# Attention: row maxima transposed in halves, sums of values in column blocks, sign bits scaled by ScalarE

## The chip, the core and the metric

One kernel runs on one core of a Trainium2 chip. The metric is the device time of one execution in microseconds. The core has five engines that matter here: TensorE (PE; its weight loads are the rows PEld), VectorE (DVE), ScalarE (ACT), GpSimd (POOL) and SyncE (SP, which issues DMAs). Each works through its own queue in program order and waits on semaphores for the others.

## The reference

A bucketed attention over 4 x 8 heads of 768 rows, followed by a routed layer of eight experts. The change touches attention alone.

```python
q_bits = (np.einsum('bhsd,dk->bhsk', q, proj) > 0).astype(np.int64)
k_bits = (np.einsum('bhsd,dk->bhsk', k, proj) > 0).astype(np.int64)
q_bucket = np.sum(q_bits * powers, axis=-1)      # powers = 2 ** np.arange(6)
k_bucket = np.sum(k_bits * powers, axis=-1)
mask = q_bucket[:, :, :, None] == k_bucket[:, :, None, :]
scores = scale * np.matmul(q, k.transpose(0, 1, 3, 2))
scores = np.where(mask, scores, -1000000000.0)
scores = scores - np.max(scores, axis=-1, keepdims=True)
attn = np.exp(scores)
attn = attn / (np.sum(attn, axis=-1, keepdims=True) + 1e-09)
return np.matmul(attn, v).astype(np.float32)
```

The result, as 3072 rows of 512, goes to the experts: each takes 384 rows by a greedy assignment over logits, and computes `relu(x @ w1) @ w2`.

## The kernel before

Heads are worked on in eight groups of four; a group `G` has its query, key and value tiles (`qp`, `kp`, `vp`), their f16 high parts (`qh`, `kh`, `vh`) and low parts (`ql`, `kl`, `vl`), and the operands `QA`, `KA`, `QB`, `KB` (two sets, alternating by group), in which the rows 64 to 69 hold sign bits times 4096 and rows from 96 on the row maxima. Signs of 4096 make equal buckets the only ones that count.

A head passes through two matrix products of the same scores:

- The **S pass** (`S_pass`, lines 231 to 238). For each of six blocks of 128 query rows, TensorE makes scores of 128 x 770 in a buffer of the pool `psS` (two buffers of two PSUM banks each), and VectorE reduces them to the negated maximum, a column of the tile `m6`.
- The **transposed scores** (`ST`, lines 255 to 262), one step later for use: for each of six blocks of 128 keys, in two halves of 384 queries, two matmuls (L260, L261) into a buffer of the pool `psT` (three buffers of one bank), and ScalarE's exponential into `pt`. GpSimd, for about a quarter of the blocks VectorE, subtracts the bf16 high part (`lo`, L265), and four steps later `AV` (L275 to L277) multiplies by the values, 18 matmuls.

Between them stands `m_rows` (lines 240 to 251): the six columns of `m6` are broadcast and transposed by six matmuls with an identity (L245), and ScalarE writes the rows from 96 on of `QA` from them (L246), which `ST` of that head reads. For the heads from 2 on the six matmuls go into one buffer of `psS`, between two S passes; for the heads 0 and 1 in halves into `psT` (L248 to L251).

Sign bits (`bits`, lines 130 to 143): f32 matmuls in four column blocks of 32 into a buffer of `psS`; VectorE compares with zero (L142) and scales by 8192 (L143). `moves` sends bits and operands through SyncE's DMA queue.

The sum of all values of a head (`sumv`, lines 195 to 210) is needed for rows that match nothing. For the groups 0 to 2 it is twelve matmuls of `vh` and `vl` with the constant `on` (L207); for the groups 3 to 7 VectorE first sums over blocks (`colsum`, L194, four per group) and one f32 matmul with `onf` follows (L202). ScalarE and VectorE then write `wf` (L209, L210).

The order is written out by hand. A step `t` runs `ST` half 0, the S passes due, the extras of slot `2t`, `ST` half 1, `lo`, the extras of slot `2t+1`, and `AV`; in one step of six `AV` stands at the step's start instead. `add(n, f, ...)` puts an extra into a slot, by the numbers of the table `AP`. S passes run nine steps ahead of `ST`. `m_rows` of a head stands two slots after its last S pass, which is behind the first S pass of the next head; the matmuls of `xtr` (L302, transposes of finished output for the logits) use `psT` too.

Of the kernel before, what the change touches and what calls it, by code (L numbers as in the profile page):

```python
# [8 lines left out]
F32 = mybir.dt.float32  # L9
F32R = mybir.dt.float32r  # L10
F16 = mybir.dt.float16
BF = mybir.dt.bfloat16
I32 = mybir.dt.int32
AF = mybir.ActivationFunctionType
# [9 lines left out]
 MR=2,  # L24
# [9 lines left out]
 EA=[(0,0),(0,0),(307,4)],  # L34
 RV=[14,3],
 MV=[28, 59, 96, 1],
 CL=9,
 WS=-23,
 SU=14,
 OPS='b0 i3 i2 t0 b1 w5 r0 r2 w4 s0 w4 C1 r1 t1 c1 s1 B0 c0 D0 w2 w1 s4 w5 s2 s3 r3 v2 w5 v0 l0 l1 C0 m0 s5 w3 s6 r5 w2 l3 e0 e1 d0 u0 u1 s7 v1 l2 w0 m1 e2 | s8 | x0 | w0 | x1 s9 | r4 s10 | | | s11 m2 v3 f0 | x3 | | x2 | m3 | | | | | |')  # L40
# [4 lines left out]
def attention(tc, nc, ctx, qT, kT, vv, proj, wg, x_dram, L, jp, identf, B, late=None, after=None):  # L45
# [64 lines left out]
    wc=row(97,768.0,"wc"); ml=row(98,-1.0,"ml")  # L110
    on=cp.tile([128,128],F16,name="on"); G_.memset(on,0.0); G_.memset(on[:,97:99],1.0)
    onf=cp.tile([128,128],F32,name="onf"); late=[lambda: G_.memset(onf,0.0),lambda: G_.memset(onf[:,97:99],1.0)]+list(late or ())
    ident=cp.tile([128,128],F16,name="ident"); V.tensor_scalar(ident,jp,0.0,None,op0=ALU.is_equal)
# [16 lines left out]
    def bits(G,pairs):  # L130
        if (G,'b') not in TMP: TMP[G,'b']=dp.tile([128,S],F16,name="bt",bufs=1)
        bt=TMP[G,'b']; r=slice(0,128)
        ps=psS.tile([128,2,512],F32,name="pss")
        for hf in range(2):
            if G==0:
                for w in range(2):
                    T.matmul(ps[32*w:32*w+32,hf,0:384],pr[0:64],(qd,kd)[w][0:64,1,hf*384:hf*384+384],start=True,stop=True,tile_position=(0,32*w))
            for p in pairs:
                for w in range(2):
                    cg=64*p+32*w  # L140
                    T.matmul(ps[cg:cg+32,hf,0:384],pr,LD[G][w][:,p,hf*384:hf*384+384],start=True,stop=True,tile_position=(0,cg))
        V.tensor_scalar(bt.rearrange("p (z q) -> p z q",z=2),ps[:,:,0:384],0.0,0.5,op0=ALU.is_gt,op1=ALU.subtract)  # L142
        V.tensor_scalar(bt[r],bt[r],8192.0,None,op0=ALU.mult)  # L143
    def dm(G,pairs,eng=SY):
# [45 lines left out]
    def sv(G,j,e=None): (e or V).tensor_tensor(VL[G%2][:,j],LD[G][2][:,j],VH[G%2][:,j,:,0:64],op=ALU.subtract)  # L190
    SV={}
    def colsum(G,j):
        if j==0: SV[G]=dp.tile([128,4,64],F32,name="sv",bufs=1)
        V.reduce_sum(SV[G][:,j],LD[G][2][:,j].rearrange("p c d -> p d c"),axis=AX.X)  # L194
    def sumv(G):
        u=G%2
        if G<2:
            A.copy(WF[u][96:128,:,64],wc[96:128,:].to_broadcast([32,4]))
        ps=psT.tile([128,512],F32,name="pst")
        pv=ps[96:128,0:256].rearrange("p (j d) -> p j d",j=4)  # L200
        pa=ps[:,0:256].rearrange("p (j d) -> p j d",j=4)
        if G in SV: T.matmul(pa,onf,SV[G],start=True,stop=True)  # L202
        else:
            n=0
            for c in range(6):
                for src in (VH[u],VL[u]):
                    T.matmul(pa,on,src[:,:,c,0:64],start=n==0,stop=n==11,skip_group_check=True); n+=1  # L207
        hi=dp.tile([128,4,64],F16,name="shi",bufs=1)
# [31 lines left out]
    def m_rows(h,hf):  # L240
        G,j=divmod(h,4)
        if h>=2:
            ps=psS.tile([128,2,512],F32,name="pss")
            for c in range(6):
                T.matmul(ps[:,c//3,c%3*128:c%3*128+128],M6[h][:,c:c+1].to_broadcast([128,128]),ident,start=True,stop=True)  # L245
            A.activation(QA[G%2][96:128,j,:].rearrange("p (z q) -> p z q",z=2),ps[96:128,:,0:384],AF.Relu,bias=mbi[96:128],scale=msc[96:128])  # L246
            return
        MR[hf]=psT.tile([128,512],F32,name="pst")  # L248
# [68 lines left out]
    def add(n,f,*a): at.setdefault(n,[]).append((f,a))  # L317
# [9 lines left out]
    for o in AP['OPS'].split():  # L327
# [3 lines left out]
        if o[0]=='e': early.append(int(o[1:]))  # L331
    add(AP['WS'],wsplit); add(AP['SU'],sumv,0)
    for G in range(1,NG):
# [5 lines left out]
        for n in range(4): add(p[8+n],sub,G,n%2,n//2)  # L339
        add(p[12],bits,G,[0,1]); add(AP['MV'][G-1] if G<4 else 48*(G-1)+AP['MV'][3],moves,G)  # L340
        for j in range(4): add(p[15]+st*j,cv,G,j); add(p[15]+st*j+sg,sv,G,j,G_)
        if G>2:
            for j in range(4): add(p[18]-AP['RV'][0]+AP['RV'][1]*j,colsum,G,j)
        add(p[18],sumv,G)
        if G>1: add(48*(G-1)+AP['CL'],clear,G)

    k=12; done={}; S_at={}
    for t in range(6*NH):
        while k<min(6+(AP['S'][0]*t+AP['S'][1])//6,t+1+LEAD,6*NH):
            S_at.setdefault(t,[]).append(divmod(k,6)); done[k//6]=t; k+=1  # L350
    for h in range(2,NH):
        add(2*done[h]+AP['MR'],m_rows,h,0)
    for h in range(1,NH,2):
# [5 lines left out]
        if after and d==3:  # L359
            for i,f in enumerate(after(b,lambda: psT.tile([128,512],F32,name="pst"),lambda: psV.tile([128,512],F32,name="psv"))):  # L360
                add(n+5 if b==B-1 else max(n+8,AP['EA'][b][0])+AP['EA'][b][1]*i,f)
    for n,f in enumerate(late): add(AP['L0'][0]+AP['L0'][1]*n,f)
    for n in sorted(x for x in at if x<0):
# [557 lines left out]
```

## Time and profile before

| | us |
|---|---|
| median of 3 runs (745.44 to 748.26) | 746.78 |
| the profiled execution | 749.0 |
| its span, first to last instruction | 747.2 |
| TensorE busy | 672.5 (90%) |
| VectorE busy | 538.3 (72%) |
| ScalarE busy | 463.5 (62%) |
| GpSimd busy | 520.0 (70%) |

All durations below are of the profiled execution, whose 749.0 us hold the span of 747.2. The busy share is a mean over attention (to about 401 us), the first assignment and the experts. Matmuls are pipelined: a matmul is listed with its whole length, while the next one starts long before its end, so that idle time is shown only where the last listed end lies ahead of the next start.

### The profile page before, as it was taken

To read this page: it belongs to the slowest core of one execution; us is meant where nothing else is said; L and a number is where in the kernel's file an instruction comes from. 1 tells how busy PE (TensorE), PEld (TensorE's weight loads), DVE (VectorE), ACT (ScalarE), POOL (GpSimd) and SP (SyncE) were. 2 spreads that over 40 slices of the span, in tenths; PEclk is the share of its full clock that TensorE was granted. 3 is DMA by queue.
4 is the path that set the end of the run, shared out by engine and by line. 5 is a ranking of instruction groups with operands and counts; after the bars stand their busy time and mean duration, and the time that the engine had idled before them with its cause. 6 is when DMAs were issued, how large, how long until landed. Compare 5 with 4: busy or idle time off the path is not lost. (4 is left out here: it accounts for less than half of the span.)

```text
span 747.2 us, 18933 instructions
## 1 busy us (share of the span) xinstructions
PE 672.5 (90%) x7739; PEld 433.1 (58%) x7739; DVE 538.3 (72%) x1150; ACT 463.5 (62%) x854; POOL 520.0 (70%) x466
## 2 busy tenths in 40 slices
PE   8989999989999899997997689999799999999995
PEld 2657666767667676675775544545345455555552
DVE  4977878988977879789955658586668878844120
ACT  7678775767767677675662181837456566666660
POOL 8588969998979889785772436565628383867671
PEclk9999999999999999999998589999999999999998
DMA  7539655427445274430000343526170717162611
GB/s 191 167 96 234 158 156 126 124 76 182 120 112 139 75 175 127 89 78 24 23 23 24 117 153 107 190 89 222 30 266 30 268 44 268 55 244 68 249 48 42
DMA packets 39950, 93.55 MB, mean 125 GB/s; under 512 B 4548, under 2 KB 30520, under 8 KB 37816
## 3 DMA queue, kind: packets, MB, share of 16 engines
q1 hardware_dynamic: 33048, 46.21, 23.6%
q0 software_dynamic: 6816, 46.15, 17.4%
q8 instruction: 60, 0.98, 0.5%
q14 instruction: 26, 0.21, 0.1%
HBM read 59.53 MB, written 12.58 MB: 97 GB/s over the span
## 5 line engine op out<-in xcount | busy, mean ns | idle before, releaser
L265 POOL TENSOR_TENSOR lo<-pt 128x768 f16<-128x768 f32 x143 | 232.6, 1641 | 48.5 <-ACT pt L262 41.9
L262 ACT ACTIVATE pt<-pst 128x384 f32<-128x384 f32 x384 | 183.0, 492 | 90.9 <-PE pst L261 75.2
L238 DVE TENSOR_REDUCE m<-pss 128x1 f16<-128x770 f32 x192 | 182.5, 956 | 37.3 <-PE pss L236 35.9
L260 PE MATMUL pst<-qa,ka 128*128 128x384 f16 x384 | 125.1, 326 | 4.2 <-ACT pt L262 2.2
L261 PE MATMUL pst<-qb,kb 128*128 128x384 f16 x384 | 124.9, 325 | 0.0
L277 PE MATMUL psv<-vh,lo 128*128 128x65 f16 x1152 | 120.9, 194 | 2.1 <-POOL lo L265 2.1
L276 PE MATMUL psv<-vl,pt 128*128 128x64 f16 x1152 | 121.2, 193 | 0.0
L275 PE MATMUL psv<-vh,pt 128*128 128x65 f16 x1152 | 121.1, 194 | 0.0
L275 PEld LDWEIGHTS <-pt 128*128 128x128 bf16 x1152 | 106.7, 98 | 12.8 <-issue 3.1
L276 PEld LDWEIGHTS <-pt 128*128 128x128 bf16 x1152 | 105.8, 99 | 9.6
L236 PE MATMUL pss<-ka,qa 128*128 128x385 f16 x384 | 94.6, 328 | 16.2 <-DVE m L238 15.6
L277 PEld LDWEIGHTS <-lo 128*128 128x128 f16 x1152 | 105.8, 97 | 2.5 <-POOL lo L265 2.5
L744 ACT ACTIVATE wh<-wf 128x1024 f16<-128x1024 f32 x64 | 67.3, 1051 | 43.9 <-DMA wf<-in_w_dram,zwidx 37.0
L756 POOL TENSOR_TENSOR wl<-wf,wh 128x512 f16<-128x512 f32 x71 | 80.0, 1147 | 0.0
L794 PEld LDWEIGHTS <-wh 128*128 128x128 f16 x512 | 48.3, 98 | 39.1 <-issue 9.9
L745 ACT ACTIVATE wf<-wf 128x1024 f32<-128x1024 f32 x62 | 65.5, 1057 | 2.0
L797 DVE SCALAR_TENSOR_TENSOR hl<-px,hh 128x384 f16<-128x384 f32 x64 | 34.4, 552 | 43.2 <-ACT hh L796 42.8
L236 PEld LDWEIGHTS <-qa 128*128 128x128 f16 x384 | 37.2, 97 | 46.6 <-issue 23.8
L265 DVE TENSOR_TENSOR lo<-pt 128x768 f16<-128x768 f32 x49 | 62.7, 1280 | 1.5 <-ACT pt L262 1.0
L806 PEld LDWEIGHTS <-hh 128*128 128x128 f16 x384 | 36.4, 98 | 39.8 <-issue 1.7
L809 ACT ACTIVATE o<-po 128x512 f32<-128x512 f32 x24 | 14.2, 592 | 70.5 <-PE po L806 70.3
L794 PE MATMUL px<-xh,wh 128*128 128x384 f16 x256 | 54.5, 331 | 2.5 <-DVE xl L770 1.4
(256 smaller groups left out, 1320.9 us busy)
## 6 DMA issues: line engine op xcount, KB each, us to landing
vp<-in_vv_dram SPq DMA_DIRECT2D x8, 768.0 KB
x_dram<-X SPq DMA_DIRECT2D x16, 384.0 KB
qp<-in_qT_dram SPq DMA_DIRECT2D x7, 768.0 KB
kp<-in_kT_dram SPq DMA_DIRECT2D x7, 768.0 KB
qa<-qh SPq DMA_DIRECT2D x14, 192.0 KB
ka<-kh SPq DMA_DIRECT2D x14, 192.0 KB
qb<-qh SPq DMA_DIRECT2D x14, 192.0 KB
kb<-kh SPq DMA_DIRECT2D x14, 192.0 KB
```

Source lines behind the costliest of these rows:

```text
L236: T.matmul(ps[:,hf,0:HK],QA[u][:,j,qc*128:qc*128+128],KA[u][:,j,hf*HK:hf*HK+HK],start=True,stop=True)
L238: V.tensor_reduce(M6[h][:,qc:qc+1],ps[:,:,0:HK],axis=AX.XY,op=ALU.max,negate=True)
L260: T.matmul(ps[:,0:384],KA[u][:,j,kr],QA[u][:,j,r],start=True,stop=False)
L261: T.matmul(ps[:,0:384],KB[u][:,j,kr],QB[u][:,j,r],start=False,stop=True)
L262: A.activation(PT[h,kc][0][:,r],ps[:,0:384],AF.Exp,scale=0.125)
L265: eng.tensor_tensor(l,p,p.bitcast(BF)[:,1::2],op=ALU.subtract)
L275: T.matmul(av[:,c,:],ph[:,r],VH[u][:,j,kc,:],start=(kc==0 and c==0),stop=False,skip_group_check=True)
L276: T.matmul(av[:,c,0:64],ph[:,r],VL[u][:,j,kc,:],start=False,stop=False,skip_group_check=True)
L277: T.matmul(av[:,c,:],l[:,r],VH[u][:,j,kc,:],start=False,stop=False,skip_group_check=True)
L744: s.nc.scalar.mul(h[:,r],f[:,r],WSC)
L756: for _ in range(n): s.nc.gpsimd.tensor_tensor(*s.pend.pop(0)[1],op=ALU.subtract)
L794: T.matmul(p[:,0:384],a[:,o:o+128],b[:,d],start=n==0,stop=n==11)
```

## The change

Row maxima: for every head `m_rows` now works in halves of three blocks, each in a buffer of `psT`. The first half goes a slot and a half after the third S pass of the head (`half`), the second two slots after the sixth, where the whole stood. `psS` is left to S passes and sign bits.

Sums: `colsum` is gone. In every group twelve matmuls with a constant of 32 columns of ones go in turn to the four column blocks of one bank, ScalarE copies the 128 x 256 partial sums to `sq`, and four slots later (`SW`; three in group 0) `sumw` sums the partitions by the f32 matmul, and writes `wf` as before. Group 0's sum moves one slot ahead.

Bits: from group 1 on, the scaling by 8192 is done by ScalarE (`bscale`), two slots after `bits`; L143 stays for group 0.

Constants: `on` and `onf` are set at the start; the list `late` is shorter by two and starts in the same slot.

```diff
- RV=[14,3],
+ SW=4,
+ BS=2,
- SU=14,
+ SU=13,
...
-    on=cp.tile([128,128],F16,name="on"); G_.memset(on,0.0); G_.memset(on[:,97:99],1.0)
-    onf=cp.tile([128,128],F32,name="onf"); late=[lambda: G_.memset(onf,0.0),lambda: G_.memset(onf[:,97:99],1.0)]+list(late or ())
+    on=cp.tile([128,32],F16,name="on"); G_.memset(on,1.0)
+    onf=cp.tile([128,128],F32,name="onf"); G_.memset(onf,0.0); G_.memset(onf[:,97:99],1.0/32)
...
-        V.tensor_scalar(bt[r],bt[r],8192.0,None,op0=ALU.mult)
+        if G==0: V.tensor_scalar(bt[r],bt[r],8192.0,None,op0=ALU.mult)
+    def bscale(G): A.mul(TMP[G,'b'],TMP[G,'b'],8192.0)
...
-    SV={}
-    def colsum(G,j):
-        if j==0: SV[G]=dp.tile([128,4,64],F32,name="sv",bufs=1)
-        V.reduce_sum(SV[G][:,j],LD[G][2][:,j].rearrange("p c d -> p d c"),axis=AX.X)
+    SQ={}
     def sumv(G):
...
+        n=0
+        for c in range(6):
+            for src in (VH[u],VL[u]):
+                g=32*(n%4)
+                T.matmul(ps[g:g+32,0:256].rearrange("p (j d) -> p j d",j=4),on,src[:,:,c,0:64],start=n<4,stop=n>7,skip_group_check=True,tile_position=(0,g)); n+=1
+        SQ[G]=dp.tile([128,256],F32,name="sq",bufs=1)
+        A.copy(SQ[G],ps[:,0:256])
+    def sumw(G):
+        u=G%2
+        ps=psT.tile([128,512],F32,name="pst")
+        T.matmul(ps[:,0:256],onf,SQ[G],start=True,stop=True)
         pv=ps[96:128,0:256].rearrange("p (j d) -> p j d",j=4)
-        pa=ps[:,0:256].rearrange("p (j d) -> p j d",j=4)
-        if G in SV: T.matmul(pa,onf,SV[G],start=True,stop=True)
-        else:
-            n=0
-            for c in range(6):
-                for src in (VH[u],VL[u]):
-                    T.matmul(pa,on,src[:,:,c,0:64],start=n==0,stop=n==11,skip_group_check=True); n+=1
         hi=dp.tile([128,4,64],F16,name="shi",bufs=1)
...
     def m_rows(h,hf):
         G,j=divmod(h,4)
-        if h>=2:
-            ps=psS.tile([128,2,512],F32,name="pss")
-            for c in range(6):
-                T.matmul(ps[:,c//3,c%3*128:c%3*128+128],M6[h][:,c:c+1].to_broadcast([128,128]),ident,start=True,stop=True)
-            A.activation(QA[G%2][96:128,j,:].rearrange("p (z q) -> p z q",z=2),ps[96:128,:,0:384],AF.Relu,bias=mbi[96:128],scale=msc[96:128])
-            return
         MR[hf]=psT.tile([128,512],F32,name="pst")
...
-        add(2*done[h]+AP['MR'],m_rows,h,0)
+        add(2*half[h]+AP['MR']+1,m_rows,h,0); add(2*done[h]+AP['MR'],m_rows,h,1)
```

On TensorE, where a head's maxima are transposed in the middle of attention (`pss` is a buffer of `psS`, `pst` of `psT`; the number is that of the tile): before, the whole stands between two S passes in a `pss` buffer.

```order
L236 MATMUL pss_4498<-ka0_168,qa0_167 128x385
L245 LDWEIGHTS m6_4245
L245 MATMUL pss_4502<-ident_201,m6_4245 128x128
...
L260 MATMUL pst_4510<-qa0_167,ka0_168 128x384
...
L260 MATMUL pst_4518<-qa0_167,ka0_168 128x384
...
L236 MATMUL pss_4522<-ka0_168,qa0_167 128x385
```

And after the change at the same place of the same head, where only the second half is left there; lines 239, 247 and 257 are the former 236, 245 and 260.

```order
L239 MATMUL pss_4566<-ka0_168,qa0_167 128x385
L247 LDWEIGHTS m6_4305
L247 MATMUL pst_4570<-ident_202,m6_4305 128x128
...
L257 MATMUL pst_4575<-qa0_167,ka0_168 128x384
...
L257 MATMUL pst_4583<-qa0_167,ka0_168 128x384
...
L239 MATMUL pss_4587<-ka0_168,qa0_167 128x385
```

The `pss` buffer between the two S passes is gone; the first half stands in `pst_4438`, ahead of a block of `AV` and two more S passes.

On VectorE, between the sixth reduction of one head and the first ones of the next in group 4, before: reductions L238, column sums L194, `lo` L265, the output's scaling L289 to L292.

```order
L238 TENSOR_REDUCE m_3751<-pss 128x1 x2
L194 TENSOR_REDUCE sv<-vp 128x64
L238 TENSOR_REDUCE m_3751<-pss 128x1
L265 TENSOR_TENSOR lo<-pt 128x768
L194 TENSOR_REDUCE sv<-vp 128x64
L238 TENSOR_REDUCE m_3751<-pss 128x1
L289 TENSOR_SCALAR r_3973<-psv 128x6
```

And after it, where the reductions are L241 and `lo` is L262:

```order
L241 TENSOR_REDUCE m_3803<-pss 128x1 x3
L262 TENSOR_TENSOR lo<-pt 128x768
L241 TENSOR_REDUCE m_3803<-pss 128x1
L286 TENSOR_SCALAR r_4024<-psv 128x6
L287 RECIPROCAL r_4024<-r_4024 128x6
```

Between `lo` and the sixth reduction nothing is left.

On ScalarE in group 1's preparation (casts of `qp` and `kp`, exponentials), before, where the third head's maxima (L246) stand behind them:

```order
L127 CAST kh<-kp 128x384
L262 ACTIVATE pt<-pst 128x384 x7
L246 ACTIVATE qa_167<-pss,mbi,msc 32x768
L262 ACTIVATE pt<-pst 128x384 x2
L189 CAST vh_209<-vp 128x6x64
```

And after it, where L259 is the exponential, L248 a half of the maxima and L145 the scaling of the bits:

```order
L128 CAST kh<-kp 128x384
L259 ACTIVATE pt<-pst 128x384 x2
L145 ACTIVATE bt<-bt 128x768
L248 ACTIVATE qa_167<-pst,mbi,msc 32x384
L259 ACTIVATE pt<-pst 128x384 x5
L248 ACTIVATE qa_167<-pst,mbi,msc 32x384
```

The scaling of group 1's bits now stands in ScalarE's queue, behind two exponentials.

## Rows read from the trace of the kernel before

**Rows 1.** View of windows; columns: stretch, its length, each engine's busy us, clock, DMA

```profile
core 0: us, PE busy (x) PEld busy (x) DVE busy (x) ACT busy (x) POOL busy (x), PEclk, DMA share, GB/s
126.00:200.00 74.00, 69.44 (x1093) 51.47 (x1092) 64.57 (x89) 54.38 (x120) 68.87 (x69) 1.00 0.50 131
126.00:395.00 269.00, 250.10 (x3951) 185.24 (x3950) 226.54 (x314) 187.16 (x396) 222.53 (x177) 1.00 0.39 99
```

**Rows 2.** View of waits, TensorE, 126 to 395 us: us in total, times, longest

```profile
PE pss L236 <- DVE m L238: 12.0, 22, 1.5
PE pss L245 <- DVE m L238: 5.2, 7, 1.8
PE pst L260 <- DVE XT L304: 0.8, 1, 0.8
```

**Rows 3.** Timeline of TensorE, three places: start us, us, engine, line, operation

```profile
71.12 0.33 PE L260 MATMUL pst<-qa,ka 128*128 128x384 f16 x1
...
197.00 0.49 PE L245 MATMUL pss<-ident,m 128*128 128x128 f16 x6 [0.94 <-DVE m L238]
...
221.26 0.49 PE L236 MATMUL pss<-ka,qa 128*128 128x385 f16 x2
...
222.41 0.33 PE L261 MATMUL pst<-qb,kb 128*128 128x384 f16 x1
222.93 0.49 PE L236 MATMUL pss<-ka,qa 128*128 128x385 f16 x2 [0.20 <-DVE m L238]
```

**Rows 4.** Timeline of VectorE around the last two places of rows 3

```profile
193.45 1.91 DVE L265 TENSOR_TENSOR lo<-pt 128x768 f16<-128x768 f32 x1
195.28 0.80 DVE L194 TENSOR_REDUCE sv<-vp 128x64 f32<-128x384 f32 x1
196.01 0.94 DVE L238 TENSOR_REDUCE m<-pss 128x1 f16<-128x770 f32 x1
...
219.54 0.95 DVE L238 TENSOR_REDUCE m<-pss 128x1 f16<-128x770 f32 x1
...
221.93 0.95 DVE L238 TENSOR_REDUCE m<-pss 128x1 f16<-128x770 f32 x1
```

**Rows 5.** Groups by line and shape: busy us, mean ns | idle before

```profile
L236 PE MATMUL pss<-ka,qa 128*128 128x385 f16 x384 | 94.6, 328 | 16.2 <-DVE m L238 15.6 <-DMA ka<-bt 0.6
...
L143 DVE TENSOR_SCALAR bt<-bt 128x768 f16<-128x768 f16 x8 | 8.9, 1119 | 0.3
...
L224 ACT CAST qb<-XT 64x768 f16<-64x768 f32 x4 | 3.3, 830 | 1.7 <-DMA XT<-in_qT_dram 1.6
```

**Rows 6.** Timeline of ScalarE at 49 and 221 us

```profile
49.65 0.49 ACT L262 ACTIVATE pt<-pst 128x384 f32<-128x384 f32 x1 [0.16 <-PE pst L261]
...
221.79 0.49 ACT L262 ACTIVATE pt<-pst 128x384 f32<-128x384 f32 x1 [1.51 <-PE pss L236]
```

**Rows 7.** Timeline of TensorE at the sign bits of one group

```profile
206.68 0.51 PE L141 MATMUL pss<-qp,pr 128*32 128x384 f32 x1
...
206.70 0.51 PE L141 MATMUL pss<-kp,pr 128*32 128x384 f32 x1
207.03 0.49 PE L141 MATMUL pss<-qp,pr 128*32 128x384 f32 x1
...
207.69 0.49 PE L141 MATMUL pss<-kp,pr 128*32 128x384 f32 x1
208.11 0.20 PE L275 MATMUL psv<-vh,pt 128*128 128x65 f16 x1
```

**Rows 8.** Timeline of SyncE's queue, three DMA issues of two groups

```profile
49.69 0.75 SPq L171 DMA_DIRECT2D qa<-bt  x1
...
62.73 0.71 SPq L185 DMA_DIRECT2D qb<-ql  x1
...
99.40 0.87 SPq L185 DMA_DIRECT2D qb<-ql  x1
```

**Rows 9.** Timeline of GpSimd at 105 us, the idle time in brackets

```profile
105.02 1.65 POOL L129 TENSOR_TENSOR ql<-qp,qh 128x768 f16<-128x768 f32 x1 [6.18 <-ACT pt L262]
```

More of the change, by code (lines that the diff above doesn't have):

```diff
@@ L331, in attention @@
         if o[0]=='e': early.append(int(o[1:]))
-    add(AP['WS'],wsplit); add(AP['SU'],sumv,0)
+    add(AP['WS'],wsplit); add(AP['SU'],sumv,0); add(AP['SU']+3,sumw,0)
     for G in range(1,NG):
@@ L339, in attention @@
         for n in range(4): add(p[8+n],sub,G,n%2,n//2)
-        add(p[12],bits,G,[0,1]); add(AP['MV'][G-1] if G<4 else 48*(G-1)+AP['MV'][3],moves,G)
+        add(p[12],bits,G,[0,1]); add(p[12]+AP['BS'],bscale,G); add(AP['MV'][G-1] if G<4 else 48*(G-1)+AP['MV'][3],moves,G)
         for j in range(4): add(p[15]+st*j,cv,G,j); add(p[15]+st*j+sg,sv,G,j,G_)
-        if G>2:
-            for j in range(4): add(p[18]-AP['RV'][0]+AP['RV'][1]*j,colsum,G,j)
-        add(p[18],sumv,G)
+        add(p[18],sumv,G); add(p[18]+AP['SW'],sumw,G)
         if G>1: add(48*(G-1)+AP['CL'],clear,G)
-    k=12; done={}; S_at={}
+    k=12; done={}; half={}; S_at={}
     for t in range(6*NH):
@@ L350, in attention @@
             S_at.setdefault(t,[]).append(divmod(k,6)); done[k//6]=t; k+=1
+            if k%6==3: half[k//6]=t
     for h in range(2,NH):
-        add(2*done[h]+AP['MR'],m_rows,h,0)
+        add(2*half[h]+AP['MR']+1,m_rows,h,0); add(2*done[h]+AP['MR'],m_rows,h,1)
     for h in range(1,NH,2):
@@ L361, in attention @@
                 add(n+5 if b==B-1 else max(n+8,AP['EA'][b][0])+AP['EA'][b][1]*i,f)
-    for n,f in enumerate(late): add(AP['L0'][0]+AP['L0'][1]*n,f)
+    for n,f in enumerate(late or ()): add(AP['L0'][0]+AP['L0'][1]*n,f)
     for n in sorted(x for x in at if x<0):
```

## The prediction

> **What bounds the kernel now.** I read the windows first [rows 1]. From 126 to 395 us, where six of the eight head groups are computed, TensorE is busy 250 of 269 us at a granted clock of 1.00 (the 2.4 GHz level) [rows 1]; VectorE is busy 226.5, ScalarE 187.2, GpSimd 222.5. TensorE works in program order, so a microsecond in which it waits there is a microsecond of the end, if nothing else takes the wait over. Next, who it waits for [rows 2]: in this stretch 22 times for a reduction `m` before an S pass (12.0 us) and 7 times before the transposing matmuls of line 245 (5.2 us), little else. The third look is one such place in the timeline [rows 3]. Line 245 takes a score buffer between two S passes. There are two, so the S pass behind it (222.93) needs the buffer of the S pass just ahead of it (221.26), whose reduction runs from 221.93 to 222.88 [rows 4]. Nothing else was late. The row shows 0.20 us of idleness, but its matmul starts 0.52 us after the one before (222.41), where two matmuls of an S pass stand 0.16 apart; matmuls overlap, and each wait is 0.16 longer than its row. So the 22 waits cost 12.0 + 22 x 0.163 = 15.6 us, and the 7 cost 5.2 + 7 x 0.163 = 6.3 us: 21.9 us that this change can reach.
>
> **Row maxima in halves.** The score buffers now hold S passes and sign bits alone. An S pass then needs the reduction of the S pass two before it, which ended over a microsecond earlier at the place shown. I expect all 22 waits to go: **-15.6 us**. The waits behind sign bits are of the same kind: there the bits' buffer adds VectorE's second pass over the bits, 1.1 us each [rows 5], which goes to ScalarE.
>
> The halves don't change the number of matmuls. The second half still follows the next head's first S pass and needs the reduction of the sixth one, so the 7 waits stay, except for what VectorE did ahead of them. At one of them (197.00) a column sum of 0.80 us stood before the reduction [rows 3, 4]; in the trace four of the seven have one, and the change removes it. That takes 0.8 + 0.5 + 0.8 + 0.8 = **-2.9 us** (the second is only 0.5 long); 3.4 stay.
>
> The first half is a new wait, for the third reduction. It stands one and a half steps behind its S pass: two score halves (0.33 each), one block of value matmuls (0.54), an S pass (0.33) and another score half, 1.9 us in all, where a reduction that starts at once ends 1.3 us after the pass. Only where a `lo` of 1.91 us stands in the way, as at 193.45 [rows 4], is it late. Behind it in TensorE's queue stand the value matmuls. Bounds: 0 and the 6.3 us that the like waits cost now. I take **+1.0**.
>
> A half also takes one of three single banks, which the score halves use. The nearest row is the transposes of the output, which take such a bank for a ScalarE copy and a VectorE subtraction: once a score half waited 0.8 us for one of those [rows 2]. A wait under the overlap of 0.16 shows no idleness, so each may hide up to that; with half of it 60 halves cost 4.8 us, with none 0. A half keeps its bank shorter, for one ScalarE operation. The tightest place is the step shown: after a score half, S pass, half and another score half stand 0.83 us of TensorE work, against 0.49 us of exponential that starts at once, since ScalarE had been idle 1.51 us before it [rows 6]. I take **+1.5**.
>
> **Column blocks.** Until now five groups used one f32 matmul behind VectorE's sums, three groups used twelve f16 matmuls. Now all eight use twelve matmuls in four column blocks, and the f32 matmul four slots later. The five groups pay the twelve extra. The sign bits already use column blocks: four matmuls start within 0.02 us of each other, the next four 0.33 us on [rows 7], though each is as long as a matmul of 384 columns in two passes. So twelve of 256 f16 columns cost three rounds of 0.11 = 0.33 us, plus what entering and leaving costs: the value matmul behind the bits starts at 208.11, 0.42 after the last one where 0.32 was due, and entering costs as much. That is 0.53 us; five times **+2.65**. Were the blocks not to overlap, 12 x 0.11 = 1.32 and five times 6.6.
>
> The Trainium skill (TensorEngine Tiling (Array Packing), section Key Properties) says that a change of tiling mode drains TensorE. The trace agrees in kind, with 0.1 us per change [rows 7]. If each drain cost the whole 0.5 us that one of these matmuls lasts, an estimate by that page and that row, five groups would pay 5 x 1.33 = 6.65 us and the end would be 4.0 us later than forecast.
>
> VectorE loses 20 column sums (0.8 us each) and seven scalings (1.1 each), some 24 us; apart from the 2.9 us above this is off the path. ScalarE gains seven scalings (0.83 by the nearest row, a cast of 768 columns [rows 5]), eight copies of 256 columns and nothing from the halves; some 9 us into 269 - 187 of idle time, at nothing. What it costs if that cover is gone is the ring above.
>
> **Before 126 us I expect nothing.** Eight such waits lie there, 15.6 - 12.0 = 3.6 us by the rows [rows 2, 5], 4.9 with the overlap, but other things end last. In the second group the scaled bits go out first in SyncE's queue: today at 49.69 [rows 8]. On ScalarE the scaling stands behind the exponential that ends at 50.14 [rows 6], so they leave 0.9 to 1.4 us later, and with them all DMAs behind (loads, `qb`, `kb` and their low parts). The last low part is issued at 62.73 [rows 8]. In the next group one issued at 99.40 [rows 8] has landed 5.6 us later; by that this one lands after 68 us, behind two whole loads perhaps later, and the fifth head's scores need it at 71.12 [rows 3]. So what is saved before 71 us is about given back. Then GpSimd stands still for 6.18 us until 105.02 [rows 9]: the row names ScalarE, which had long been done; what it writes, `ql`, is one buffer, and the DMA issued at 99.40 reads that. TensorE then waits for `lo` behind it. Bounds: -4.9 and +1.0; I take 0. GpSimd may also be late after 126; +1.0 for that.
>
> **Sum**: -15.6 - 2.9 + 1.0 + 1.5 + 2.65 + 1.0 = -12.35 us. Against the profiled execution's own 749.0 us (span 747.2) this gives 736.7; its time is 2.2 above the median of 746.8, so on the median **734.5 us**. What follows attention (routing, experts) isn't touched and moves up as a whole.
>
> **Rivals.**
> - *GpSimd sets the pace.* From 126 to 200 us it is busy 68.9 of 74, over the whole stretch 222.5 of 269 [rows 1]. If of the 5.1 us that are idle up to 200 only a third is usable (the rest it waits for its input), that stretch's part of the 15.6 us, 74/269 or 4.3, yields 1.7, and the rest loses about 2 more; the gain is near 7.7: 739. Against it: after 126 TensorE never waits for GpSimd [rows 2]. 0.15.
> - *The single banks become the wait, slower.* If every half holds a score half up for a whole exponential (0.49 us), 60 of them cost 29.4 instead of 1.5: 762. It ends slower than before from 13.85 / 60 = 0.23 us per half. For it: three banks for two score halves and one half in each such step; against it the 0.83 us of work to 0.49 above. 0.06.
> - *The transfers set the pace, no change.* Each later group's `ql` must land before GpSimd takes the next, as at 105.02 [rows 9]; if the chain of DMAs ended last in every group as it does there, steps could not shorten, and 2 us would be left: 745. Against it: after 126 the waits of GpSimd name inputs from ScalarE and VectorE, no landing. 0.10.
> - *All waits go*, a part of the early ones too, and the banks cost nothing: 21.9 + 2 - 2.65 = 21, or 726. 0.09.
>
> **How the numbers follow.** The forecast's own spread, 729 to 739, has 0.60. The range 728 to 742 adds most of the first rival and leaves out the two slow cases and half of the last. A measurement of this kernel can tell about 0.5%, 3.7 us, from no change. Faster by more (under 743.1): 0.60 + 0.09 + 0.13 = 0.82; slower by more 0.06; the rest, 0.12, within.
>
> **What would show it.** Right: no S pass waits for `m` behind line 245's successor; the first halves wait under 2 us in all; four column blocks start within 0.02 us; the stretch from 126 on is 12 us shorter while the stretch before isn't. Wrong: score halves that wait for ScalarE or VectorE right behind a half (banks); value matmuls that wait for `lo` after 126 (GpSimd); GpSimd standing still for `ql` in each group (transfers); column blocks that start 0.11 us apart.

## The result

| | before | after |
|---|---|---|
| median of four runs, us | 747.0 (745.44 to 748.26) | 738.57 (736.18 to 740.49) |
| profiled execution, us | 749.0 | 736.18 |
| its span, us | 747.2 | 734.4 |

The ratio is 0.9873, with a 95% interval from 0.9843 to 0.9902: faster by 1.3%, or 8.4 us by the medians, 12.8 us by the two profiled executions. The forecast said 734.5 on the median (range 728 to 742) and 736.7 for the profiled execution.

One measure is used from here on, since the change touches attention alone: **the stretch from the tenth head on**, between the starts of TensorE's first score matmul of the tenth head and of the last head's last one. Before they stand at 132.90 and 396.44, after at 133.41 and 386.36:

```profile
133.41 0.33 PE L257 MATMUL pst<-qa,ka 128*128 128x384 f16 x1
...
386.36 0.32 PE L257 MATMUL pst<-qa,ka 128*128 128x384 f16 x1
```

That is 263.5 us before and 252.9 after, 10.6 us less. It starts 0.5 us later: attention ends 10.1 us earlier. The other 2.7 us between the profiled executions lie behind attention, in the assignment and the experts, which the change doesn't touch; at one place there, from 441.4 to 444.6 us, the profile of before shows the granted clock at 0.50 (1.2 GHz), right after a microsecond in which TensorE was busy 0.19, and the profile of after stays at 1.00 at the same work. At half the clock those 3.2 us can hold at most 1.6 of the 2.7; where the rest comes from isn't settled. So 12.8 is the change and luck, 8.4 has an uncertainty of 2.2, and 10.1 is what the trace shows.

### The profile page after: what moved, and what is told of

It is laid out like the page before. It is cut to its first block, busy times and chain, and to the rows that moved or that the text cites. A ratio compares the mean times of both kernels' runs of the same rounds, so it can differ in the third digit from the quotient of the medians.

```text
span 734.4 us, 19117 instructions
## 1 busy us (share of the span) xinstructions
PE 672.9 (92%) x7805; PEld 430.7 (59%) x7805; DVE 512.8 (70%) x1123; ACT 481.0 (66%) x899; POOL 519.1 (71%) x465
## 5 line engine op out<-in xcount | busy, mean ns | idle before, releaser
L262 POOL TENSOR_TENSOR lo<-pt 128x768 f16<-128x768 f32 x143 | 229.9, 1622 | 40.7 <-ACT pt L259 32.6
L259 ACT ACTIVATE pt<-pst 128x384 f32<-128x384 f32 x384 | 181.7, 491 | 71.4 <-PE pst L258 61.0
L241 DVE TENSOR_REDUCE m<-pss 128x1 f16<-128x770 f32 x192 | 182.1, 957 | 48.9 <-PE pss L239 47.8
L262 DVE TENSOR_TENSOR lo<-pt 128x768 f16<-128x768 f32 x49 | 55.4, 1131 | 1.5 <-ACT pt L259 1.0
L790 PE MATMUL px<-xh,wl 128*128 128x384 f16 x256 | 53.7, 327 | 0.3 <-POOL wl L752 0.3
```

Source lines behind the costliest of these rows:

```text
L241: V.tensor_reduce(M6[h][:,qc:qc+1],ps[:,:,0:HK],axis=AX.XY,op=ALU.max,negate=True)
L259: A.activation(PT[h,kc][0][:,r],ps[:,0:384],AF.Exp,scale=0.125)
L262: eng.tensor_tensor(l,p,p.bitcast(BF)[:,1::2],op=ALU.subtract)
L790: T.matmul(p[:,0:384],a[:,o:o+128],b[:,d],start=n==0,stop=n==11)
```

## The profile after

The windows answer to [rows 1]: TensorE is busy 253.1 us where it was 250.1 (the column blocks came), but of 260 us instead of 269. VectorE lost 19 us, ScalarE gained 13:

```profile
core 0: us, PE busy (x) PEld busy (x) DVE busy (x) ACT busy (x) POOL busy (x), PEclk, DMA share, GB/s
126.00:386.00 260.00, 253.13 (x4034) 186.14 (x4032) 207.64 (x292) 199.84 (x431) 222.02 (x176) 1.00 0.40 103
```

The view of TensorE's waits in the same window (us in total, times, longest) answers to [rows 2]:

```profile
PE pst L257 <- ACT qa L248: 3.1, 5, 0.7
PE pst L257 <- DVE XT L301: 2.4, 2, 1.3
PE pst L247 <- DVE m L241: 0.7, 3, 0.2
PE pst L257 <- ACT pt L259: 0.3, 1, 0.3
```

S passes (now line 239) no longer appear: the 22 waits are gone. At the place of [rows 3] S pass, half, score halves and S pass now follow each other in 0.16 to 0.33 us steps:

```profile
217.97 0.49 PE L239 MATMUL pss<-ka,qa 128*128 128x385 f16 x2
218.30 0.33 PE L247 MATMUL pst<-ident,m 128*128 128x128 f16 x3
218.47 0.33 PE L257 MATMUL pst<-qa,ka 128*128 128x384 f16 x1
...
219.12 0.49 PE L239 MATMUL pss<-ka,qa 128*128 128x385 f16 x2
```

The transposing matmuls (now 247) wait three times, 0.7 us in all, against seven times and 5.2. New is the first row: five times a score half waits for a row-maxima half, which the prediction had named as the sign of the banks. The second row, score halves behind the transposes of the output, has grown from 0.8.

The new wait, on TensorE, ScalarE and VectorE (start, us, engine, line, operation; the idle time in brackets). It is the step in which the f32 sum (209) and the second half (247) stand together:

```profile
252.32 0.59 PE L209 MATMUL pst<-sq,onf 128*128 128x256 f32 x2
252.75 0.33 PE L247 MATMUL pst<-ident,m 128*128 128x128 f16 x3
252.92 0.33 PE L257 MATMUL pst<-qa,ka 128*128 128x384 f16 x1
253.08 0.33 PE L258 MATMUL pst<-qb,kb 128*128 128x384 f16 x1
254.06 0.32 PE L257 MATMUL pst<-qa,ka 128*128 128x384 f16 x1 [0.65 <-ACT qa L248]
```

```profile
252.95 0.36 ACT L212 CAST shi<-pst 32x256 f16<-32x256 f32 x1 [0.21 <-PE pst L209]
253.34 0.66 ACT L248 ACTIVATE qa<-pst,mbi,msc 32x384 f16<-32x384 f32 x1
```

```profile
252.77 0.95 DVE L241 TENSOR_REDUCE m<-pss 128x1 f16<-128x770 f32 x1
253.75 0.49 DVE L213 SCALAR_TENSOR_TENSOR wf<-shi,ml,pst 32x256 f16<-32x256 f16 x1
```

Three banks, one of them with the score half of 252.92, and at 253.24 the next score half wants one. The f32 sum's bank is read twice, by ScalarE until 253.31 and by VectorE, which has a reduction to finish first, until 254.24. So the half's bank comes free first, at 254.00. The starts are 0.98 us apart where 0.16 is usual: a wait of 0.81 us, the same in four groups, 0.69 in the last.

The column blocks answer to [rows 7]:

```profile
200.97 0.49 PE L239 MATMUL pss<-ka,qa 128*128 128x385 f16 x2
201.40 0.28 PE L203 MATMUL pst<-vh,on 128*32 128x256 f16 x1
...
201.41 0.28 PE L203 MATMUL pst<-vl,on 128*32 128x256 f16 x1
201.52 0.27 PE L203 MATMUL pst<-vh,on 128*32 128x256 f16 x1
...
201.85 0.34 PE L257 MATMUL pst<-qa,ka 128*128 128x384 f16 x1
```

Four start within 0.01 us, the next four 0.11 later; the next score half follows 0.88 after the start of the S pass. Of that 0.33 are the S pass itself, by the distances of the starts, so that all twelve with entering and leaving cost 0.55 us.

## Experiments

Each kernel's time was compared with runs of the kernel before beside it (747.0 to 747.7 us). "Stretch" is the one from the tenth head on; waits are excesses over the usual distance of two starts, from 126 us on, as in the prediction. Stretch and waits are those of one profiled execution per kernel; how much the stretch of one kernel varies between executions, no run here shows. The diffs show the lines that matter; `...` stands for those left out.

| kernel | median us | ratio to before, 95% | stretch us | S passes wait | transposing matmuls wait |
|---|---|---|---|---|---|
| before | 747.0 | | 263.5 | 15.6 | 6.3 |
| after | 738.6 | 0.9873 (0.9843 to 0.9902) | 252.9 | 0 | 1.2 |
| halves alone | 743.2 | 0.9934 (0.9907 to 0.9961) | 258.0 | 0 | 10.1 |
| sums alone | 744.6 | 0.9960 (0.9939 to 0.9981) | 258.1 | 12.2 | 1.7 |
| bits alone | 746.0 | 0.9978 (0.9954 to 1.0003) | 260.5 | 11.4 | 4.9 |
| halves undone | 742.1 | 0.9942 (0.9918 to 0.9965) | 256.1 | 8.8 | 1.7 |
| sums undone | 739.5 | 0.9899 (0.9865 to 0.9933) | 255.7 | 0 | 7.2 |
| bits undone | 746.8 | 0.9981 (0.9948 to 1.0014) | 256.7 | 0 | 4.5 |

### One part alone

**The halves alone**, on the kernel before:

```diff
...
-        add(2*done[h]+AP['MR'],m_rows,h,0)
+        add(2*half[h]+AP['MR']+1,m_rows,h,0); add(2*done[h]+AP['MR'],m_rows,h,1)
```

> The kernel before with the halves alone; sums and sign bits as before. Theory (the gain is the score buffer that line 245 took): the 22 S pass waits go here too (15.6 us), the sums on VectorE keep about half of the 6.3 us of waits of the transposing matmuls, no column blocks are paid (about 3.7 us in the changed kernel) and no bank is shared with the f32 sum (4 us): about 16 to 18 us under the kernel before, near 730, and faster than the whole change. Rival (VectorE's relief by the sums and the scaling is the gain): most waits of S passes stay, at best 4 us are won. Rival (GpSimd sets the pace): as the whole change, 8 to 10 us, with waits for lo.

My theory fell. The 22 waits did go, but the stretch shrank by 5.5 us and the median by 3.8, not 16: the halves wait themselves.

```profile
PE pst L244 <- DVE m L238: 8.2, 10, 1.7
PE pst L254 <- DVE XT L298: 3.5, 5, 1.3
```

One such place, TensorE and VectorE:

```profile
259.69 0.28 PE L244 MATMUL pst<-ident,m 128*128 128x128 f16 x2
260.87 0.23 PE L244 MATMUL pst<-ident,m 128*128 128x128 f16 x1 [0.91 <-DVE m L238]
```

```profile
258.24 1.70 DVE L259 TENSOR_TENSOR lo<-pt 128x768 f16<-128x768 f32 x1
259.86 1.82 DVE L238 TENSOR_REDUCE m<-pss 128x1 f16<-128x770 f32 x2
```

The first two columns are there; the third is the reduction at 259.86, late behind a `lo` of 1.70 us. VectorE was late before and is late here; the halves only change who meets it. The second row of the view, score halves whose bank is held until VectorE's subtraction of an output transpose is done, says the same.

**The sums alone**:

```diff
...
-        if G>2:
-            for j in range(4): add(p[18]-AP['RV'][0]+AP['RV'][1]*j,colsum,G,j)
-        add(p[18],sumv,G)
+        add(p[18],sumv,G); add(p[18]+AP['SW'],sumw,G)
```

> The kernel before with the column-block sums and the later f32 sum alone; whole row maxima in the score buffer. Theory: the 22 S pass waits stay, column sums ahead of reductions go (about 3 us won), five groups pay about 0.7 us each on TensorE (3.5 us lost): within 2 us of the kernel before. Rival (VectorE's relief is the gain): at least 5 us faster than before. Rival (the column blocks cost more than sized): over 3 us slower.

The stretch is 5.4 us shorter, by the rival's number, though the median is only 2.4 lower. S passes still wait 20 times, but for less, and the transposing matmuls hardly:

```profile
PE pss L237 <- DVE m L239: 8.7, 20, 1.0
PE pss L246 <- DVE m L239: 0.9, 3, 0.3
```

**The scaling alone**:

```diff
...
-        V.tensor_scalar(bt[r],bt[r],8192.0,None,op0=ALU.mult)
+        if G==0: V.tensor_scalar(bt[r],bt[r],8192.0,None,op0=ALU.mult)
+    def bscale(G): A.mul(TMP[G,'b'],TMP[G,'b'],8192.0)
...
```

> The kernel before with the scaling of the sign bits on ScalarE alone. Theory: nothing on the path, within 1 us of the kernel before; the start of the fifth head's scores (71.1 us before, 71.7 after) moves by at most 0.9 us later. Rival (VectorE's relief is the gain): 2 to 7 us faster (seven scalings of 1.1 us, reductions queued behind them). Rival (the later bits delay the transfers): 1 to 3 us slower, all of it before 126 us.

The time can't be told from no change, but the stretch is 3.0 us shorter: the rival again. It holds two delays that the stretches of before and after don't have. At 292.16 a score half waits 2.0 us for an exponential; ScalarE had just stood idle for 3.09 us ahead of a cast of `kp`. And from 345.0 to 348.4 us the granted clock was 0.50, after 5 us in which TensorE was busy 2.63; there two steps are 1.2 us longer than before.

```profile
PE pst L262 <- ACT pt L264: 2.6, 2, 1.8
```

So 3.0 is what is left beside those delays, and whether they belong to the edit isn't shown. This profiled execution began 7 us late, before the first head, so the start of the fifth head's scores can't be compared; the first nine heads took 109.1 us against 109.4 before.

Alone, the parts take 5.5, 5.4 and 3.0 us off the stretch, 14.0 in all, together 10.6. They draw on the same waits.

### One part undone

**The halves undone**: the whole row maxima back in a score buffer, sums and scaling as after.

```diff
...
-        add(2*half[h]+AP['MR']+1,m_rows,h,0); add(2*done[h]+AP['MR'],m_rows,h,1)
+        add(2*done[h]+AP['MR'],m_rows,h,0)
```

> The changed kernel with the row maxima whole again, in a score buffer between two S passes; the sums in column blocks and the scaling on ScalarE stay. Theory (the halves are worth something of their own even with VectorE relieved): S passes wait for a reduction again some 20 times, 8 to 12 us in all; the shared step of half and f32 sum (4.4 us) and the waits behind the transposes of the output (1.7 us more than before) go; the stretch from the tenth head on is 256 to 259 us (changed kernel 252.9), the kernel 3 to 6 us slower than the changed one. Rival (VectorE's relief was all that was missing, the halves only cost banks): S pass waits under 4 us, stretch under 252, faster than the changed kernel.

As expected, at the lower end: 256.1 us, 742.1 in all. Relief of VectorE takes the waits of S passes from 15.6 to 8.8, and the halves are needed for the rest.

```profile
PE pss L239 <- DVE m L241: 5.9, 17, 0.6
PE pss L248 <- DVE m L241: 1.0, 3, 0.4
```

**The sums undone** (the diff of the sums, backwards):

> The changed kernel with the sums undone: VectorE's column sums and one f32 matmul again for the groups 3 to 7, halves and the scaling on ScalarE kept. Measure: the stretch from the tenth head's first transposed scores to the last ones (before 263.5 us, changed kernel 252.9, halves alone 258.0). Theory now (VectorE is late at some places, and the wait goes to whoever needs its reduction next; the sums bring relief of VectorE at the price of TensorE time): waits of the halves come back, 4 to 8 us in all, column blocks (about 3.5 us) and the shared step (4 us) go: about equal to the changed kernel, 251 to 255 us. Rival (the halves' place alone decides, relief is worth nothing): no wait of a half over 0.5 us, and the stretch is 7 us shorter, near 246. Rival (relief is everything): the whole loss of the halves alone comes back, 257 or more.

255.7 us, just above the theory's band. The halves' waits came back, 7.2 us against 1.2; that is 6.0 more, a little less than the 6.7 that column blocks (2.8) and shared step (3.9) had cost. Other waits make it longer all the same: three score halves and four halves, 2.3 us in all, held up at output transposes, and three score halves, 0.7, that wait for an exponential.

```profile
PE pst L246 <- DVE m L240: 5.8, 7, 1.7
```

**The scaling undone**:

> The changed kernel with the scaling of the sign bits on VectorE again. Theory (relief of VectorE where S passes wait behind sign bits): the S pass behind sign bits waits again up to 1 us in the groups 3 to 7, the stretch from the tenth head on is 2 to 4 us longer than the changed kernel's 252.9; the stretch ahead of it is up to 0.9 us shorter, since the scaled bits leave earlier. Rival (ScalarE's scaling holds an exponential up and costs as much): within 1 us of the changed kernel.

256.7 us, 3.8 longer, at the upper end. What waits is not the S pass behind the sign bits, as I had written, but the first half of four heads, 0.8 to 0.9 us each, and once a value matmul, 0.7. The median is 8.2 us above that of the changed kernel, so that by the median the whole gain is gone; in the trace 3.8 of that lie before the tenth head. There GpSimd stands still for 10.13 us for a landing (last section), TensorE then waits 4.99 us for `lo`, until 112.20, and the granted clock is at 0.50 from 109.7 to 116.5. Why GpSimd waits longer here was not settled, and with one profile it isn't shown that the edit is the cause.

**Relief without column blocks**: the halves alone, with the column sums left out.

```diff
-            V.reduce_sum(SV[G][:,j],LD[G][2][:,j].rearrange("p c d -> p d c"),axis=AX.X)
+            V.memset(SV[G],0.0)
```

> The kernel before with the halves, and VectorE's column sums left out (one small memset per group stands in their place, so the rows that match nothing get a wrong sum): it parts VectorE's relief from the cost of the column blocks. Halves alone: stretch from the tenth head on 258.0 us with 10.1 us of waits of the transposing matmuls. Theory (those waits come from the column sums of 0.8 us, four per group, ahead of reductions): under 4 us of them are left, stretch 251 to 253. Rival (they come from lo on VectorE and the halves' place): 8 us or more are left, stretch over 256.

251.4 us against 258.0 with the sums, as by the theory; 735.3 us in all, ratio 0.9837 (0.9804 to 0.9870). The waits fell from 10.1 to 4.7 us, a little more than I had left for them; four, 2.8 us, are first halves, of the same four heads as with the scaling undone: in both kernels VectorE scales the bits. So 6.6 us is what twenty column sums of 0.8 us cost once the halves are there.

### The price of the sums and the banks

**Full width**: the twelve matmuls over 128 columns.

```diff
...
-                T.matmul(ps[g:g+32,0:256].rearrange("p (j d) -> p j d",j=4),on,src[:,:,c,0:64],start=n<4,stop=n>7,skip_group_check=True,tile_position=(0,g)); n+=1
+                T.matmul(ps[:,0:256].rearrange("p (j d) -> p j d",j=4),on,src[:,:,c,0:64],start=n==0,stop=n==11,skip_group_check=True); n+=1
```

> The changed kernel with the twelve sum matmuls over all 128 columns, one after the other in one accumulation, in place of four column blocks. Theory (four blocks run at once; three rounds of 0.11 us and 0.4 us of entering and leaving): twelve times 0.11 = 1.32 us in place of about 0.75, so 0.6 us more in each of the groups 3 to 7, stretch from the tenth head on about 255.8 us, kernel 3 us slower than the changed one. Rival (each change of tiling drains TensorE for half a microsecond, so blocks gain nothing): equal or up to 2 us faster than the changed kernel, value matmuls behind the sums starting 0.11 after the last one.

The matmuls start 0.11 us apart:

```profile
203.77 0.27 PE L202 MATMUL pst<-vh,on 128*128 128x256 f16 x1
203.88 0.27 PE L202 MATMUL pst<-vl,on 128*128 128x256 f16 x1
...
205.09 0.32 PE L256 MATMUL pst<-qa,ka 128*128 128x384 f16 x1
```

From 203.77 to 205.09 it is 1.32 us in place of 0.55, five times 0.77 = 3.9 us; the stretch is 3.9 longer (256.9). The kernel took 743.7 us, ratio 0.9955 (0.9934 to 0.9976).

**The f32 sum moved** out of the step of the second half:

```diff
-        add(p[18],sumv,G); add(p[18]+AP['SW'],sumw,G)
+        add(p[18],sumv,G); add(p[18]+(2 if G>2 else AP['SW']),sumw,G)
```

> The changed kernel with the f32 sum of the groups 3 to 7 two slots earlier, so that it no longer stands in one step with the second half of the row maxima. Theory (three single banks for two score halves, one half and one sum are one too few, 0.81 us each time): the five waits of 0.81, 0.81, 0.81, 0.81 and 0.69 us go, attention ends about 3.9 us earlier than in the changed kernel and the kernel takes about 734.5. Rival (the exponentials or GpSimd set the pace there, and the wait only shows where the sum stands): the same as the changed kernel within 1 us, with waits of the same size elsewhere.

The five waits are gone from the view:

```profile
PE pst L257 <- DVE XT L301: 2.4, 2, 1.3
PE pst L247 <- DVE m L241: 0.7, 3, 0.2
```

The stretch is 250.0 us, 2.9 shorter, not 3.9: 0.7 came back as three waits of 0.24 behind S passes, for exponentials, and 0.2 at an output transpose. 736.6 us, ratio 0.9845 (0.9813 to 0.9876), the fastest but for the one without column sums, though its interval overlaps with that of the changed kernel.

**A further tenant of a bank** (a small result that takes one for a while), in 18 steps of that kernel:

```diff
+    def tenant():
+        ps=psT.tile([128,512],F32,name="pst")
+        for z in range(2): T.matmul(ps[:,z*128:z*128+128],ident,ident,start=True,stop=True)
+        A.copy(TEN,ps[:,0:256])
...
+        if 12<=h<30: add(2*done[h]+AP['MR'],tenant)
```

> The kernel with the moved f32 sum, and in 18 steps a further tenant of a single bank ahead of the second half: two matmuls with the identity and a ScalarE copy of 256 columns that nothing reads. It measures what the rival of the single banks would have cost. Theory (two score halves and one half fill the three banks, a further tenant costs what the f32 sum did): 0.8 us each, 14 us, and 2 us of matmuls; stretch from the tenth head on 264 to 267 us (moved sum 250.0). Rival (a bank that only ScalarE reads comes free in time): the 2 us of matmuls alone, 252.

The rival was nearer: 253.7 us, 3.6 more for 18 tenants. Step by step the price is a little higher than this mean of 0.20. Fifteen of the 18 steps are 0.31 us longer each; three, whose half waits for its reduction anyway, are not, and one wait of 1.3 us behind an output transpose, which the kernel with the moved sum has, isn't there. One of the fifteen:

```profile
254.72 0.49 PE L239 MATMUL pss<-ka,qa 128*128 128x385 f16 x2
255.06 0.27 PE L245 MATMUL pst<-ident 128*128 128x128 f16 x2
255.17 0.33 PE L252 MATMUL pst<-ident,m 128*128 128x128 f16 x3
255.53 0.32 PE L262 MATMUL pst<-qa,ka 128*128 128x384 f16 x1
```

The tenant's matmuls take 0.11 of the 0.31; the score half at 255.53 then waits 0.2. That is a quarter of 0.81, for a bank that ScalarE alone reads, so the number of tenants doesn't explain the 0.81.

**One reader for the f32 sum**, left in its step:

```diff
...
-        A.copy(hi[96:128],pv)
-        V.scalar_tensor_tensor(WF[u][96:128,:,0:64],hi[96:128],ml[96:128],pv,op0=ALU.mult,op1=ALU.add)
+        A.copy(sw[96:128],pv)
+        A.copy(hi[96:128],sw[96:128])
+        V.scalar_tensor_tensor(WF[u][96:128,:,0:64],hi[96:128],ml[96:128],sw[96:128],op0=ALU.mult,op1=ALU.add)
```

> The changed kernel, the f32 sum left in the step of the second half, but its bank is read by ScalarE alone: one copy of 256 columns to a tile, from which the f16 part and VectorE's operation then take their data (one ScalarE copy more, five times, some 0.4 us each). Theory now (a bank is dear when VectorE reads it behind a reduction of 0.95 us; a further bank that only ScalarE reads cost 0.2 us in the kernel with the tenants): the five waits of 0.81 and 0.69 us shrink to 0.2 to 0.4 us each, the stretch from the tenth head on is 250 to 251.5 us (changed kernel 252.9). Rival (four banks wanted in one step are one too many, whoever reads them): waits of 0.8 us or more, since ScalarE has one copy more, stretch 253 to 255.

Half right. The score half inside the step waits 0.1 us instead of 0.81, so VectorE's read was the cause of that wait. But the stretch stays at 252.8, because ScalarE's queue is now late, here with its extra copy (214), the half (250) and the scaled bits (145) between the exponentials (261):

```profile
256.86 0.36 ACT L213 COPY sw<-pst 32x256 f32<-32x256 f32 x1 [0.21 <-PE pst L209]
257.26 0.40 ACT L214 CAST shi<-sw 32x256 f16<-32x256 f32 x1
257.56 0.66 ACT L250 ACTIVATE qa<-pst,mbi,msc 32x384 f16<-32x384 f32 x1
258.25 0.49 ACT L261 ACTIVATE pt<-pst 128x384 f32<-128x384 f32 x1
258.76 0.84 ACT L145 ACTIVATE bt<-bt 128x768 f16<-128x768 f16 x1
```

TensorE waits for it 0.47 us in each of the five groups (the 0.1, and 0.35 at a later score half), 0.24 more in three of them; with three smaller waits elsewhere that is 3.8 us, against 3.9 in the changed kernel. The time is 740.8 us, ratio 0.9902 (0.9871 to 0.9932).

**Two further moves** on the kernel with the moved sum:

```diff
- X=[2, 2, 5],
+ X=[2, 2, 6],
...
- SU=13,
+ SU=14,
...
-        add(p[18],sumv,G); add(p[18]+(2 if G>2 else AP['SW']),sumw,G)
+        e=(0,4,2)[G] if G<3 else 0; add(p[18]+e,sumv,G); add(p[18]+e+2,sumw,G)
...
-        for hf in range(2): add(n+AP['X'][1]*hf,xtr,b,d,hf)
+        for hf in range(2): add(n+(3 if h<NH-1 else 2)*hf,xtr,b,d,hf)
```

> The kernel with the moved f32 sum; in addition the second of two output transposes stands half a step later, and the sums of the groups 0 to 2 stand half a step to two steps later, with their f32 sums two slots behind. Theory for the first: the waits of 1.27 and 1.51 us behind output transposes in the last batch go, stretch from the tenth head on near 247.5 us (moved sum 250.0). Theory for the second (GpSimd and the transfers behind it set the pace of the first groups): the 5 us of waits for vl go, but waits for lo take their place, and the tenth head starts within 1 us of the moved sum's 133.9. Rival for the second (TensorE's wait for vl is time lost): the tenth head starts 3 to 5 us earlier. Kernel about 734 by the theories, about 730 by the rival.

No gain: 738.0 us, ratio 0.9895 (0.9865 to 0.9924). The transposes of the output now wait themselves (1.4 us once, for the same subtraction), and the stretch is 251.3. The early sums came out nearer to the theory: the idle time for `vl` fell from 4.0 to 0.7 us, others took its place, and the tenth head starts 109.0 us after the first, against 110.0. (`X` moves the logits half a step with the transposes, `SU` the sum of group 0.)

## Why the prediction was right, and where not

**The mechanism and the sum.** Of the 10.6 us, by the distances of TensorE's starts in the stretch, beside the prediction's terms (from 126 us on):

| step of the prediction | predicted us | trace us |
|---|---|---|
| S passes | -15.6 | -15.2 (all 21 that lie in the stretch) |
| transposing matmuls, second half | -2.9 | -5.2 |
| first half's new wait | +1.0 | 0 |
| single banks | +1.5 | +6.6 (f32 sum's step 3.9, output transposes 2.3, one wait for an exponential 0.4) |
| column blocks | +2.65 | +2.8 |
| GpSimd late | +1.0 | 0 |
| not booked | | +0.4 |
| sum | -12.35 | -10.6 |

That the sum lies only 1.8 us off is partly luck: the banks cost 5.1 us more than forecast, and three other terms, the second halves, the first halves and GpSimd, came out 4.3 us better. That the profiled execution, 736.2, met the forecast of 736.7 is luck too: 2.7 of its 12.8 us lie behind attention.

**S passes.** Right. The buffer of line 245 was what they waited for, and no reduction takes its place at an S pass.

**Column blocks.** Right: 0.55 us against 0.53 by [rows 7]. Were they not to overlap, I had 1.32, and the full width measured just that. The Trainium skill (TensorEngine Tiling (Array Packing), section Key Properties) says that a change of tiling mode drains TensorE. The trace agrees in kind: the first block starts 0.26 us after an S pass's last matmul, where a full-width sum starts 0.17 after it, and leaving costs 0.10; the half microsecond per drain that I set against it as an estimate isn't there.

**The banks.** The term that failed in size, +1.5 against 6.6, beyond its bound of 4.8. I had sized it by the halves, which cost next to nothing. The five shared steps weren't looked at: the order shows the f32 sum in the step of the second half, and what that bank waits for is VectorE behind a reduction, 0.8 us each. The nearest row, a wait of 0.8 us for the subtraction of a transpose [rows 2], had the right kind and size; I counted halves instead of banks that VectorE reads. Outside the shared steps the halves cost nothing that shows: with a first half between, two score halves start 1.03 us apart where it was 0.87, and the 0.17 is missing again at the old place.

**VectorE's relief.** "Apart from the 2.9 us this is off the path" was wrong. The runs show relief and halves as one thing: without the relief the halves wait 10.1 us, where the forecast's terms give 6.3 + 1.0; with it 1.2. So the relief took 8.9 us off the path and not 2.9, and the first halves, forecast at 1.0, cost 4.9 of the 10.1 without it and nothing with it. Undoing the sums costs 2.7 us of the stretch even though it saves column blocks and shared steps; undoing the scaling costs 3.8. The second halves lost 5.2 and not 2.9 us for the same reason.

**Before the tenth head.** Nothing was expected, and that came true, but on another path. The 0.5 us is lost before the first head's scores, which start at 24.02 us against 23.54; the nine heads then take 109.4 us in both. The scaled bits do leave SyncE's queue later, at 51.15 against 49.69 [rows 8], 1.5 us (0.9 to 1.4 forecast), but the fifth head's scores, at 71.69 against 71.12, start only 0.1 us later counted from the first head's.

```profile
51.15 0.75 SPq L173 DMA_DIRECT2D qa<-bt  x1
```

Much of what the S passes save there goes into a wait that the prediction didn't have: the sums of the groups 0 to 2 wait for GpSimd's `vl`, first before, then after:

```profile
PE pst L207 <- POOL vl L190: 0.3, 1, 0.3
```

```profile
PE pst L203 <- POOL vl L192: 4.2, 3, 2.1
```

The kernel of the two further moves shows that this wait isn't what ends last there: without most of it only 1.0 us is won. The wait of [rows 9] now names its cause itself:

```profile
105.92 1.64 POOL L130 TENSOR_TENSOR ql<-qp,qh 128x768 f16<-128x768 f32 x1 [5.94 <-DMA qb<-ql]
```

**The rivals.** The time by the median, 738.6, lies near the 739 of "GpSimd sets the pace", but that didn't happen: in the stretch no matmul waits for `lo`. "The transfers set the pace" holds before the tenth head only, where the prediction had counted on it. "The single banks, slower" needed 0.23 us per half; that is about what a tenant waited, 0.2, but the halves outside the shared steps cost nothing that shows. "All waits go" was nearly right on the waits, of which 1.2 us are left, and lost to the price of the sums and the banks.

## What to carry over

When a wait names one engine at many places, ask whether that engine is late or only the buffer short: here a buffer alone moved half of the waits (21.9 us) to the next one who needed the late result, and work taken off that engine removed the rest. So an edit tried alone tells little about its share: alone the three parts took 5.5, 5.4 and 3.0 us off the stretch, together 10.6. Before a small operation is put into a ring of banks, list who reads each bank and what stands ahead of the reader in its queue: one read by a lightly used engine cost a wait of 0.2 us here, one by VectorE behind a reduction 0.8. And compare parts by a stretch of the trace that holds the change, since the rest of this kernel varies by more than the parts are worth.

## What I had not expected

The idle time of GpSimd for the landing of `ql` in the fourth group varied from 4.5 to 10.1 us over the fourteen profiled executions. The first nine heads took 109.0 to 114.3 us, and the two longest of these times, 113.2 and 114.3, go with the two longest waits, 10.1 and 9.2. The longest wait:

```profile
109.09 1.64 POOL L130 TENSOR_TENSOR ql<-qp,qh 128x768 f16<-128x768 f32 x1 [10.13 <-DMA qb<-ql]
```

That one is of the kernel with the scaling undone. These are fourteen different kernels, so it isn't shown that this landing also makes up part of the 3 to 11 us by which runs of one kernel differ; what delays it was not tried.

`lo` on VectorE, always the same 128 x 768 elements, takes 0.95 us at its fastest and up to 2.35 in the profile of before. Of the 19 there that take over 1.2 us, 17 run while GpSimd is busy throughout, of the 30 others 2. Its mean over 49 was 1.28 us before, 1.13 after and 1.36 with the halves alone, as in this row of its groups:

```profile
L259 DVE TENSOR_TENSOR lo<-pt 128x768 f16<-128x768 f32 x49 | 66.4, 1356 | 1.5 <-ACT pt L256 1.0
```

The long ones stand just ahead of the reductions that come late, so part of VectorE's lateness may come from GpSimd's work beside it. No run here separates the two.
